# Layers multiplied in couples of 64 rows, one per half of the tokens, with each unit's second turn behind the next unit's first

## The chip, the cores and the metric

The kernel runs on one core of one Trainium2 chip. The metric is the device time of one execution in microseconds (us). The median of 3 runs of the kernel before is 607.14 us (607.09 to 607.23).

Engines are named as in the profile: PE is TensorE's matrix multiplier and PEld its loading of weights, DVE is VectorE, ACT is ScalarE, POOL is GpSimd, and SP is the engine whose queue issues the DMAs here.

## The reference

A causal attention is followed by two layers with gates and squares. In short, with batch 2, 12 heads, 448 positions, head size 64, so 896 tokens of 768 channels:

```
scores = q @ k.T / sqrt(64), masked above the diagonal
attn   = exp(scores - max) / (sum + 1e-9)
x      = attn @ v, as 896 x 768
g      = x @ w_gate                      # 768 x 1536
y      = (g * sigmoid(g) * (x @ w_val)) @ w_out      # 1536 x 768
h      = y @ w_in                        # 768 x 2048
out    = (max(h, 0) ** 2) @ w_out2       # 2048 x 768
```

q, k and v are float32; the weights are float64 and are read from memory as pairs of 32-bit words.

## The kernel before

The attention comes first (lines 655 to 662). Its order on all engines is written by a planner (`attention_plan`), and two of its parts matter here. Lines 496 to 498 multiply the scores of two heads as a couple: one head's data lies in rows 0 to 63 of the tiles and the other's in rows 64 to 127, and each goes to a bank of its own. And the planner also splits the first weights and multiplies the first half of the tokens of units 0 and 1 early (tiles `early`, line 635).

The layers work in *units*, the list `units` of lines 287 to 297. A unit is a set of 128 x 768 weights: `g` and `v` are the gate and value weights for 128 of 1536 channels (24 units, in turns g, v, g, v), `o` is half of the contraction for 128 channels of y (12 units, two per m), `h` is 128 channels of the second hidden layer (16 units), `f` is a stretch of the last product (16 units).

For each unit, SP loads 768 KB of raw weights (`load_w`, line 319). Then `split_w` makes two float32r tiles of them, `whi` (the high part) and `wlo` (what is left of it), in nine steps: ACT takes the absolute value (L337) and copies the high part (L352), and DVE does L340, L345, L349, L355, L359, L362 and L365; the last of these writes `wlo`. L359 is the last to read the raw tile, and so frees it for another load. `split_to` interleaves the steps of one unit with the first steps of the next, and puts *follow-ups* between them: work on earlier results that waits in the list `later` (sigmoid, products, copies out of PSUM).

A product of float32 precision is three matmuls of float32r: high weights by high part of the activations, high by low, low by high (`mm3`, lines 590 to 598). Each is done for both halves of the tokens (448 each), which have a PSUM bank each. A unit of g, v, o or h is six blocks of 128 rows, so 6 x 3 x 2 = 36 matmuls of 128 rows and 448 columns. Each of them loads its weights itself. The last layer (line 766) uses the activations as weights and 384 columns, and stays as it is.

What sets the order in the layers is the order in which the code is written: on each engine instructions run as they were issued. `unit` (line 406) splits up to the next unit's weights, issues loads, and returns this unit's weights; then come its matmuls; its follow-ups are put into `later` and are issued between the steps of the next split. There are 8 PSUM banks; a bank is taken again after eight others.

Of the kernel before, what the change touches and what calls it, by code (L numbers as in the profile page):

```python
# [16 lines left out]
ALU = mybir.AluOpType  # L17
PSUM = bass.MemoryType.PSUM

# [219 lines left out]
def tile_attention_moe_moe(ctx, tc, q, k, v, w_gate, w_val, w_out, w_in2, w_out2, out):  # L239
# [17 lines left out]
    wsp_p = ctx.enter_context(tc.tile_pool(name="wsp", bufs=3))  # L257
# [32 lines left out]
    for m in range(KD):  # L290
        units += [("o", m, 0), ("o", m, 1)]
# [127 lines left out]
    def halves(b):  # L419
        return slice(b * S, (b + 1) * S)  # L420
# [178 lines left out]

    def gate_or_val(kind, m, bs):  # L600
        hi, lo = unit(kind, m, 0)
        pss = {b: bank(kind) for b in bs}
        for kk in range(KD):
            c = slice(kk * 128, (kk + 1) * 128)
            mm3(pss, hi[:, c], lo[:, c], x_hi[kk], x_lo[kk], kk == 0, kk == KD - 1)
        return pss
# [42 lines left out]
    with tc.manual_schedule():  # L649
# [43 lines left out]
        for m in range(KF1):  # L693
            for kind in "gv":
                ps = gate_or_val(kind, m, [1] if n < NEARLY else [0, 1])
                if n < NEARLY:
                    ps[0] = early[n]
                n += 1
                if kind == "g":
                    later += [partial(sigmoids, ps), *(partial(times, sg, ps[z], z) for z in range(B))]  # L700
                else:
                    later.append(lambda: None)
                    for z in range(B):
                        later += [partial(times, up, ps[z], z), partial(gated, m, z)]
# [4 lines left out]
        for m in range(KD):  # L709
            pss = {b: bank("y") for b in range(B)}  # L710
            for j in range(2):
                hi, lo = unit("o", m, j)
                n = KF1 // 2
                for kk in range(n):
                    c = slice(kk * 128, (kk + 1) * 128)
                    f = j * n + kk
                    mm3(pss, hi[:, c], lo[:, c], g_hi[f], g_lo[f], f == 0, f == KF1 - 1)

            def first_part(m, pss):
                for b in range(B):  # L720
                    nc.scalar.activation(out=y_hi[m][:, halves(b)], in_=pss[b][:, :S], func=AF.Copy)

            def rest(m, pss, b):
                hs = halves(b)
                nc.vector.tensor_tensor(
                    out=y_lo[m][:, hs], in0=pss[b][:, :S], in1=y_hi[m][:, hs].bitcast(F32),
                    op=ALU.subtract)

            later += [partial(first_part, m, pss), partial(rest, m, pss, 0), partial(rest, m, pss, 1)]
# [4 lines left out]
        for m in range(KF2):  # L734
            hi, lo = unit("h", m, 0)
            pss = {b: bank("h") for b in range(B)}
            for kk in range(KD):
                c = slice(kk * 128, (kk + 1) * 128)
                mm3(pss, hi[:, c], lo[:, c], y_hi[kk], y_lo[kk], kk == 0, kk == KD - 1)
            u = {}  # L740
# [14 lines left out]
            later += [partial(squares, m, pss, u), partial(rest, m, u, 0), partial(rest, m, u, 1)]  # L755
# [4 lines left out]
        for half in range(2):  # L760
# [17 lines left out]
            for t in range(NTK):  # L778
                o = tmp_p.tile([128, N], F32, tag="osb", name="osb", bufs=6)
                if t % 2:  # L780
                    nc.vector.tensor_copy(out=o, in_=pss[t][:, :N])
                else:
                    nc.scalar.activation(out=o, in_=pss[t][:, :N], func=AF.Copy)
                nc.sync.dma_start(
                    out=out[t * 128:(t + 1) * 128, half * N:(half + 1) * N], in_=o)
# [30 lines left out]
```

## Time and profile before

| what | value |
|---|---|
| median of 3 runs | 607.14 us |
| the profiled execution's own time | 606.39 us |
| its span, first to last instruction | 604.6 us |
| granted TensorE clock | 1.00 |
| PE busy | 598.3 us, 99% |
| DVE busy | 479.2 us, 79% |
| ACT busy | 280.0 us, 46% |
| POOL busy | 91.9 us, 15% |

The profile is of one execution. A busy PE isn't PE at its peak: matmuls are pipelined and their ends are modelled, so the time that one takes in a stream is read from the starts of two, not from its length. In the timeline a row gives start and length in us, engine, line, operation, output and inputs by the program's names, shapes and the count of equal instructions merged into the row; brackets hold the engine's idle time ahead of it and what ended this. Names of tiles are shared by several uses: `b` in a row of o or h is an activation tile, `y` is the bank that o writes.

### The profile page before, as it was taken

How to read it: one execution, taken by the hardware profiler on the slowest of the kernel's cores; microseconds unless marked ns; L12 is line 12 of the kernel's file. 1: busy time of each engine (PE TensorE's matmuls, PEld its weight loads, DVE VectorE, ACT ScalarE, POOL GpSimd, SP SyncE). 2: the span in 40 equal slices, each digit the busy share in tenths (PEclk: the TensorE clock that was granted, in tenths of full speed). 3: DMA queues.
4: the chain of work that ended last, by engine and by line, in shares of the span. 5: the costliest groups of instructions: out<-in, count | busy, mean ns of one | idle time of the engine just before them, and what ended most of it. 6: DMA issues, size and time to landing. Idle time of an engine off the chain costs nothing.

```text
span 604.6 us, 8813 instructions
## 1 busy us (share of the span) xinstructions
PE 598.3 (99%) x3257; PEld 531.7 (88%) x3258; DVE 479.2 (79%) x843; ACT 280.0 (46%) x544; POOL 91.9 (15%) x161
## 2 busy tenths in 40 slices
PE   8999999999999999999999999999999999999997
PEld 5667667999999999999999999999999999999997
DVE  4779994888999999999977776888888888649741
ACT  5889883433333333333422224666666642222201
POOL 6556573111111111111000000000000000000000
PEclk9999999999999999999999999999999999999999
DMA  7776210333333333333433333333333335345202
GB/s 162 163 195 159 84 53 2 106 104 105 104 105 105 105 105 104 105 105 107 155 105 105 104 105 105 106 105 105 105 104 106 104 106 157 104 134 139 82 1 91
DMA packets 80778, 65.05 MB, mean 108 GB/s; under 512 B 34912, under 2 KB 76640, under 8 KB 80736
## 3 DMA queue, kind: packets, MB, share of 16 engines
q1 hardware_dynamic: 80736, 64.50, 36.2%
q8 instruction: 25, 0.41, 0.3%
q14 instruction: 17, 0.14, 0.1%
HBM read 61.73 MB, written 2.75 MB: 107 GB/s over the span
## 4 chain that ended last, share of the span: by engine, by line
PE 97%; POOL 1%; DMA 0%; SPq 0%; issue 0%; DVE 0%; ACT 0%; ACTq 0%; POOLq 0%
PE o L766 19%; PE h L598 7%; PE h L596 7%; PE h L594 7%; PE y L596 5%; PE y L594 5%; PE y L598 5%; PE v L594 5%; PE g L594 5%; PE g L596 5%; PE v L596 5%; PE v L598 5%; PE g L598 5%; PE s L498 4%; PE x L573 3%; PE pt L544 3%
## 5 line engine op out<-in xcount | busy, mean ns | idle before, releaser
L352 ACT ACTIVATE whi<-wa 128x768 fp32r<-128x768 f32 x68 | 57.6, 847 | 177.6 <-DVE wa L349 135.1
L766 PE MATMUL o<-whi,b 128*128 128x384 f32 x336 | 85.6, 334 | 0.0
L340 DVE TENSOR_SCALAR wa<-wa 128x768 f32<-128x768 f32 x68 | 41.4, 608 | 45.9 <-ACT wa L337 45.9
L349 DVE SCALAR_TENSOR_TENSOR wa<-wraw,wa 128x768 uint32<-128x768 uint32 x68 | 75.6, 1112 | 0.1
L337 ACT ACTIVATE wa<-wraw 128x768 f32<-128x768 f32 x68 | 61.7, 907 | 17.8 <-DVE wlo L365 17.8
L365 DVE TENSOR_TENSOR wlo<-wa,wr 128x768 fp32r<-128x768 f32 x68 | 65.6, 965 | 0.1
L362 DVE TENSOR_TENSOR wa<-wa,whi 128x768 f32<-128x768 f32 x68 | 64.6, 950 | 0.4 <-ACT whi L352 0.4
L359 DVE SCALAR_TENSOR_TENSOR wr<-wraw,wr 128x768 f32<-128x768 uint32 x68 | 64.6, 950 | 0.0
L766 PEld LDWEIGHTS o<-whi,b 128*128 128x128 f32 x336 | 60.7, 188 | 0.0
L766 PE MATMUL o<-wlo,b 128*128 128x384 f32 x168 | 56.2, 334 | 0.0
L598 PE MATMUL h<-b,wlo 128*128 128x448 f32 x192 | 55.2, 368 | 0.0
L594 PE MATMUL h<-b,whi 128*128 128x448 f32 x192 | 55.2, 368 | 0.0
L689 POOL TENSOR_TENSOR b<-u,b 128x448 fp32r<-128x448 f32 x24 | 29.0, 1207 | 159.2 <-ACT b L688 159.2
L534 POOL TENSOR_SCALAR P<-P,st 128x448 f32<-128x448 f32 (+1 forms) x96 | 50.5, 545 | 12.2 <-DVE st L526 9.2
L516 ACT ACTIVATE P<-P,st 128x192 f32<-128x192 f32 (+3 forms) x96 | 47.6, 498 | 7.4 <-DVE st L510 4.8
L596 PE MATMUL y<-b,whi 128*128 128x448 f32 x144 | 41.4, 368 | 0.0
L598 PE MATMUL y<-b,wlo 128*128 128x448 f32 x144 | 41.4, 368 | 0.0
L594 PE MATMUL y<-b,whi 128*128 128x448 f32 x144 | 41.4, 368 | 0.0
L596 PE MATMUL g<-alo,whi 128*128 128x448 f32 x138 | 40.2, 368 | 0.0
L596 PE MATMUL v<-alo,whi 128*128 128x448 f32 x138 | 40.2, 368 | 0.0
L594 PE MATMUL v<-ahi,whi 128*128 128x448 f32 x138 | 40.2, 368 | 0.0
L594 PE MATMUL g<-ahi,whi 128*128 128x448 f32 x138 | 40.2, 368 | 0.0
(97 smaller groups left out, 1152.7 us busy)
## 6 DMA issues: line engine op xcount, KB each, us to landing
wraw<-in_moe_w_out_dram SPq DMA_DIRECT2D x28, 768.0 KB, 4.4
wraw<-in_moe_w_in_dram SPq DMA_DIRECT2D x16, 768.0 KB, 4.6
wraw<-in_moe_w_gate_dram SPq DMA_DIRECT2D x12, 768.0 KB, 4.3
wraw<-in_moe_w_val_dram SPq DMA_DIRECT2D x12, 768.0 KB, 4.4
raw<-in_q_dram SPq DMA_DIRECT2D x24, 112.0 KB, 2.7
raw<-in_k_dram SPq DMA_DIRECT2D x24, 112.0 KB, 2.9
out_dram<-osb SPq DMA_DIRECT2D x14, 192.0 KB, 1.9
v<-in_v_dram SPq DMA_DIRECT2D x24, 96.0 KB, 2.7
```

The lines of the kernel that those rows point to most:

```text
L337: nc.scalar.activation(out=af, in_=high.bitcast(F32), func=AF.Abs)
L349: nc.vector.scalar_tensor_tensor(out=a, in0=high, scalar=0xC0000000, in1=a, op0=ALU.bitwise_and, op1=ALU.bitwise_or)
L352: nc.scalar.activation(out=split_t[n][0], in_=af, func=AF.Copy)
L359: nc.vector.scalar_tensor_tensor(out=rf, in0=low, scalar=2.0 ** -52, in1=rf, op0=ALU.mult, op1=ALU.mult)
L362: nc.vector.tensor_tensor(out=af, in0=af, in1=split_t[n][0].bitcast(F32), op=ALU.subtract)
L365: nc.vector.tensor_tensor(out=split_t[n][1], in0=af, in1=r[0].bitcast(F32), op=ALU.add)
L516: nc.scalar.activation(out=a, in_=a, func=AF.Exp, scale=-1.0, bias=st(0), accum_out=st(1))
L534: nc.gpsimd.tensor_scalar(out=o, in0=a, scalar1=st(2), scalar2=1.0, op0=ALU.mult, op1=ALU.mult)
L594: nc.tensor.matmul(out=pss[b][:, :S], lhsT=hi, rhs=mhi[:, halves(b)], start=first, stop=False)
L596: nc.tensor.matmul(out=pss[b][:, :S], lhsT=hi, rhs=mlo[:, halves(b)], start=False, stop=False)
L598: nc.tensor.matmul(out=pss[b][:, :S], lhsT=lo, rhs=mhi[:, halves(b)], start=False, stop=last)
L766: nc.tensor.matmul(out=pss[t][:, :N], lhsT=a[f][:, tk], rhs=w[:, c], start=f + n == 0, stop=f == KF2 - 1 and n == 2)
```

## The change

A product of g, v, o and h is now made in two *turns*. In each turn every block of 128 rows is multiplied as couples: a matmul with rows 0 to 63 for one half of the tokens, and one with rows 64 to 127 for the other half. In turn 0 rows 0 to 63 go to the first half's bank, in turn 1 they go to the second half's. So a unit has 2 x 18 couples, 72 matmuls instead of 36, each with a load of its own. In a turn a bank is written by one half of the rows alone.

A bank changes from one half of the rows to the other between the two turns. `product` issues a unit's first turn, then a no-op on SP that waits for the turn's last two matmuls, and then the *second turn of the unit before*. The first two matmuls of a second turn wait for the no-op of their own unit. The second turn of a stage's last unit is issued at the stage's end (`second_turn()` calls).

Units 0 and 1 of g and v stay as they were. In o the units come in another order: for two m at a time, first the two units with j = 0, then the two with j = 1, and for j = 1 the first turn has the rows of j = 0's second one. There are now four buffers for split weights instead of three, and four for output tiles instead of six.

```diff
@@ -16,6 +16,7 @@
 AF = mybir.ActivationFunctionType
 ALU = mybir.AluOpType
 PSUM = bass.MemoryType.PSUM
+AFTER = mybir.DependencyInfo(mybir.DependencyClass.Sync, mybir.DependencyReason.DATA)
 
 
 W_TINY = 2.0 ** (896 // 8 - 127)
@@ -254,7 +255,7 @@
     const = ctx.enter_context(tc.tile_pool(name="const", bufs=1))
     wraw_p = ctx.enter_context(tc.tile_pool(name="wraw", bufs=3))
     dec_p = ctx.enter_context(tc.tile_pool(name="wdec", bufs=1))
-    wsp_p = ctx.enter_context(tc.tile_pool(name="wsp", bufs=3))
+    wsp_p = ctx.enter_context(tc.tile_pool(name="wsp", bufs=4))
     ax_p = ctx.enter_context(tc.tile_pool(name="ax", bufs=1))
     early_p = ctx.enter_context(tc.tile_pool(name="early", bufs=1))
     ps_p = ctx.enter_context(tc.tile_pool(name="ps", bufs=8, space=PSUM))
@@ -287,8 +288,8 @@
     units = []
     for m in range(KF1):
         units += [("g", m, 0), ("v", m, 0)]
-    for m in range(KD):
-        units += [("o", m, 0), ("o", m, 1)]
+    for m in range(0, KD, 2):
+        units += [("o", m + z, j) for j in range(2) for z in range(2)]
     for m in range(KF2):
         units.append(("h", m, 0))
     FU = KF2 // 2
@@ -597,6 +598,47 @@
         for b in bs:
             nc.tensor.matmul(out=pss[b][:, :S], lhsT=lo, rhs=mhi[:, halves(b)], start=False, stop=last)
 
+    open_turns = []
+
+    def turn(t, ws, pss, xs, first, last, ready=None):
+
+        mms = []
+        for kk, (mhi, mlo) in enumerate(xs):
+            c = slice(kk * 128, (kk + 1) * 128)
+            for z, (w, a) in enumerate(((0, mhi), (0, mlo), (1, mhi))):
+                for r in range(2):
+                    b, rows = r ^ t, slice(64 * r, 64 * r + 64)
+                    mms.append(nc.tensor.matmul(
+                        out=pss[b][:, :S], lhsT=ws[w][rows, c], rhs=a[rows, halves(b)],
+                        start=first and kk == z == 0, stop=last and kk == len(xs) - 1 and z == 2))
+        if ready:
+            for mm in mms[:2]:
+                tc.add_manual_dep(mm.ins, ready.ins.name, AFTER, reason="banks change rows")
+        return mms[-2:]
+
+    def second_turn():
+        for args, done in open_turns:
+            turn(*args)
+            later.extend(done)
+        open_turns.clear()
+
+    def product(key, pss, xs, first=True, last=True, done=()):
+
+        t, n = int(not first), units.index(key)
+        split_to(n + 2)
+        ws = split_t[n]
+        mms = turn(t, ws, pss, xs, first, False)
+        ready = nc.sync.nop()
+        for mm in mms:
+            tc.add_manual_dep(ready.ins, mm.ins.name, AFTER, reason="banks change rows")
+        load_w(n + 5)
+        second_turn()
+        open_turns.append(((1 - t, ws, pss, xs, False, last, ready), done))
+
     def gate_or_val(kind, m, bs):
         hi, lo = unit(kind, m, 0)
         pss = {b: bank(kind) for b in bs}
@@ -692,52 +734,53 @@
         n = 0
         for m in range(KF1):
             for kind in "gv":
-                ps = gate_or_val(kind, m, [1] if n < NEARLY else [0, 1])
                 if n < NEARLY:
+                    ps = gate_or_val(kind, m, [1])
                     ps[0] = early[n]
+                else:
+                    ps = {b: bank(kind) for b in range(B)}
+                if kind == "g":
+                    done = [partial(sigmoids, ps), *(partial(times, sg, ps[z], z) for z in range(B))]
+                else:
+                    done = [lambda: None]
+                    for z in range(B):
+                        done += [partial(times, up, ps[z], z), partial(gated, m, z)]
+                if n < NEARLY:
+                    later += done
+                else:
+                    product((kind, m, 0), ps, list(zip(x_hi, x_lo)), done=done)
                 n += 1
-                if kind == "g":
-                    later += [partial(sigmoids, ps), *(partial(times, sg, ps[z], z) for z in range(B))]
-                else:
-                    later.append(lambda: None)
-                    for z in range(B):
-                        later += [partial(times, up, ps[z], z), partial(gated, m, z)]
+        second_turn()
 
 
 ...
+        half = KF1 // 2
+        for m in range(0, KD, 2):
+            both = [{b: bank("y") for b in range(B)} for z in range(2)]
             for j in range(2):
-                hi, lo = unit("o", m, j)
-                n = KF1 // 2
-                for kk in range(n):
-                    c = slice(kk * 128, (kk + 1) * 128)
-                    f = j * n + kk
-                    mm3(pss, hi[:, c], lo[:, c], g_hi[f], g_lo[f], f == 0, f == KF1 - 1)
-
-            def first_part(m, pss):
-                for b in range(B):
-                    nc.scalar.activation(out=y_hi[m][:, halves(b)], in_=pss[b][:, :S], func=AF.Copy)
-
-            def rest(m, pss, b):
-                hs = halves(b)
-                nc.vector.tensor_tensor(
-                    out=y_lo[m][:, hs], in0=pss[b][:, :S], in1=y_hi[m][:, hs].bitcast(F32),
-                    op=ALU.subtract)
-
-            later += [partial(first_part, m, pss), partial(rest, m, pss, 0), partial(rest, m, pss, 1)]
+                for z, pss in enumerate(both):
+                    product(
+                        ("o", m + z, j), pss, list(zip(g_hi, g_lo))[j * half:(j + 1) * half], j == 0, j == 1,
+                        [partial(first_part, m + z, pss), *(partial(rest, m + z, pss, b) for b in range(B))]
+                        if j else [])
+        second_turn()
 
 
         free = x_hi[4:] + x_lo + extra[:24]
         r_hi, r_lo = free[0:32:2], free[1:32:2]
         for m in range(KF2):
-            hi, lo = unit("h", m, 0)
-            pss = {b: bank("h") for b in range(B)}
-            for kk in range(KD):
-                c = slice(kk * 128, (kk + 1) * 128)
-                mm3(pss, hi[:, c], lo[:, c], y_hi[kk], y_lo[kk], kk == 0, kk == KD - 1)
-            u = {}
+            pss, u = {b: bank("h") for b in range(B)}, {}
 
             def squares(m, pss, u):
                 for b in range(B):
@@ -752,7 +795,9 @@
                 nc.vector.tensor_tensor(
                     out=r_lo[m][:, hs], in0=u[b], in1=r_hi[m][:, hs].bitcast(F32), op=ALU.subtract)
 
-            later += [partial(squares, m, pss, u), partial(rest, m, u, 0), partial(rest, m, u, 1)]
+            product(("h", m, 0), pss, list(zip(y_hi, y_lo)), done=[
+                partial(squares, m, pss, u), *(partial(rest, m, u, b) for b in range(B))])
+        second_turn()
 
 
         N = DM // 2
@@ -776,7 +821,7 @@
                 for z, t in order:
                     add_up(hi, lo, u, z, t)
             for t in range(NTK):
-                o = tmp_p.tile([128, N], F32, tag="osb", name="osb", bufs=6)
+                o = tmp_p.tile([128, N], F32, tag="osb", name="osb", bufs=4)
                 if t % 2:
                     nc.vector.tensor_copy(out=o, in_=pss[t][:, :N])
                 else:

```

The functions `first_part` and `rest` of o stand ahead of its loop now, unchanged.

In the rows that follow, lines are those of the kernel they come from: after the change `turn` multiplies in L615, and the lines of the split and the follow-ups are one or some more (L366 for L365, L726 for L684).

On PE, at a border in g and v. Before: the end of a v unit (banks v_1692 and v_1693, weights whi_1588 and wlo_1589) and the start of the next g unit.

```order
L596 MATMUL v_1692<-alo5_88,whi_1588 128x448
L596 MATMUL v_1693<-alo5_88,whi_1588 128x448
L598 MATMUL v_1692<-ahi5_82,wlo_1589 128x448
L598 MATMUL v_1693<-ahi5_82,wlo_1589 128x448
L594 MATMUL g_1753<-ahi0_77,whi_1626 128x448 [waits Activation_49]
L594 MATMUL g_1754<-ahi0_77,whi_1626 128x448
L596 MATMUL g_1753<-alo0_83,whi_1626 128x448
L596 MATMUL g_1754<-alo0_83,whi_1626 128x448
L598 MATMUL g_1753<-ahi0_77,wlo_1627 128x448 [waits DVE_49]
L598 MATMUL g_1754<-ahi0_77,wlo_1627 128x448
```

After, for the border of a later pair: the end of a g unit's first turn (banks g_1956 and g_1957), the start of the second turn of the v unit before it, and its continuation.

```order
L615 MATMUL g_1956<-alo5_88,whi_1782 128x448
L615 MATMUL g_1957<-alo5_88,whi_1782 128x448
L615 MATMUL g_1956<-ahi5_82,wlo_1783 128x448
L615 MATMUL g_1957<-ahi5_82,wlo_1783 128x448
L615 MATMUL v_1859<-ahi0_77,whi_1686 128x448 [waits SP_sequencer_49]
L615 MATMUL v_1858<-ahi0_77,whi_1686 128x448
L615 MATMUL v_1859<-alo0_83,whi_1686 128x448
L615 MATMUL v_1858<-alo0_83,whi_1686 128x448
L615 MATMUL v_1859<-ahi0_77,wlo_1687 128x448
L615 MATMUL v_1858<-ahi0_77,wlo_1687 128x448
```

Where the next unit's matmuls followed, the second turn of the unit before now follows; its couples take the banks in the other order (1859 first), and its first matmul waits for SP.

On DVE, while the weights of unit 4 are split (`wlo_1627` before, `wlo_1629` after), with unit 2's follow-ups before (`sg` is made of the bank g_1633 and g_1634):

```order
L355 TENSOR_SCALAR wr_1679<-wa_1612 128x768
L340 TENSOR_SCALAR wa_1673<-wa_1673 128x768
L359 SCALAR_TENSOR_TENSOR wr_1679<-wraw_1546,wr_1679 128x768
L345 TENSOR_SCALAR wa_1673<-wa_1673 128x768
L684 TENSOR_TENSOR sg_1675<-g_1633,sg_1675 128x448
L362 TENSOR_TENSOR wa_1612<-wa_1612,whi_1626 128x768
L349 SCALAR_TENSOR_TENSOR wa_1673<-wraw_1570,wa_1673 128x768
L684 TENSOR_TENSOR sg_1677<-g_1634,sg_1677 128x448
L365 TENSOR_TENSOR wlo_1627<-wa_1612,wr_1679 128x768
```

and after, up to the follow-ups of the same unit 2 (banks g_1610 and g_1611), which now stand with unit 5's split (`wlo_1687`):

```order
L363 TENSOR_TENSOR wa_1614<-wa_1614,whi_1628 128x768
L350 SCALAR_TENSOR_TENSOR wa_1676<-wraw_1570,wa_1676 128x768
L366 TENSOR_TENSOR wlo_1629<-wa_1614,wr_1678 128x768
L356 TENSOR_SCALAR wr_1772<-wa_1676 128x768
L341 TENSOR_SCALAR wa_1766<-wa_1766 128x768
L360 SCALAR_TENSOR_TENSOR wr_1772<-wraw_1570,wr_1772 128x768
L346 TENSOR_SCALAR wa_1766<-wa_1766 128x768
L726 TENSOR_TENSOR sg_1768<-g_1610,sg_1768 128x448
L363 TENSOR_TENSOR wa_1676<-wa_1676,whi_1686 128x768
L350 SCALAR_TENSOR_TENSOR wa_1766<-wraw_1612,wa_1766 128x768
L726 TENSOR_TENSOR sg_1770<-g_1611,sg_1770 128x448
L366 TENSOR_TENSOR wlo_1687<-wa_1676,wr_1772 128x768
```

The two products of `sg` moved from ahead of unit 4's low part to ahead of unit 5's; the same holds for all later follow-ups of g and v.

## Rows read from the trace of the kernel before

**Rows 1.** The page: busy time, share of the span and instructions of each engine.

```profile
PE 598.3 (99%) x3257; PEld 531.7 (88%) x3258; DVE 479.2 (79%) x843; ACT 280.0 (46%) x544; POOL 91.9 (15%) x161
```

**Rows 2.** By stretch: length, PE, PEld, DVE, ACT, POOL busy, clock, DMA.

```profile
112.20:275.90 163.70, 163.70 (x794) 148.74 (x793) 148.32 (x200) 60.30 (x89) 26.62 (x22) 1.00 0.33 106
...
365.20:484.20 119.00, 119.00 (x578) 108.12 (x577) 98.60 (x143) 78.55 (x125) 0.00 (x0) 1.00 0.35 104
```

**Rows 3.** Timeline of PE: starts of unit 2, o and h.

```profile
112.20 0.57 PE L594 MATMUL g<-ahi,whi 128*128 128x448 f32 x2
...
275.88 0.57 PE L594 MATMUL y<-b,whi 128*128 128x448 f32 x2
...
365.16 0.57 PE L594 MATMUL h<-b,whi 128*128 128x448 f32 x2
```

**Rows 4.** Timeline of PE: three bf16 matmuls in the attention.

```profile
10.00 0.82 PE L275 MATMUL qk<-warm 128*128 128x512 bf16 x3
```

**Rows 5.** Groups by line: the same matmuls, count, busy us and mean ns.

```profile
L275 PE MATMUL qk<-warm 128*128 128x512 bf16 x7 | 2.2, 382 | 0.0
```

**Rows 6.** Timeline of PE and PEld: transposes, then the scores' couples.

```profile
62.82 0.55 PE L474 MATMUL qk<-ident,raw 112*128 112x112 f32 x4
...
63.11 0.26 PE L474 MATMUL qk<-ident,raw 112*128 112x112 f32 x1
63.30 0.19 PEld L498 LDWEIGHTS s<-qk 64*128 64x128 f32 x2
...
63.40 0.19 PEld L498 LDWEIGHTS s<-qk 64*128 64x128 f32 x2
...
63.78 0.81 PE L498 MATMUL s<-qk 64*128 64x448 f32 x4
...
64.15 0.70 PE L498 MATMUL s<-qk 64*128 64x320 f32 x4
...
64.42 0.60 PE L498 MATMUL s<-qk 64*128 64x320 f32 x4
```

**Rows 7.** Timeline of DVE in g and v: L340, two units apart.

```profile
180.78 0.83 DVE L340 TENSOR_SCALAR wa<-wa 128x768 f32<-128x768 f32 x1 [0.97 <-ACT wa L337]
...
195.57 0.82 DVE L340 TENSOR_SCALAR wa<-wa 128x768 f32<-128x768 f32 x1 [0.98 <-ACT wa L337]
```

**Rows 8.** Timeline of DVE: low parts of units 3, 23, 25, 62, 63.

```profile
117.77 1.91 DVE L365 TENSOR_TENSOR wlo<-wa,wr 128x768 fp32r<-128x768 f32 x1
...
266.55 0.94 DVE L365 TENSOR_TENSOR wlo<-wa,wr 128x768 fp32r<-128x768 f32 x1
...
281.32 0.94 DVE L365 TENSOR_TENSOR wlo<-wa,wr 128x768 fp32r<-128x768 f32 x1
...
553.02 0.95 DVE L365 TENSOR_TENSOR wlo<-wa,wr 128x768 fp32r<-128x768 f32 x1
...
554.96 0.56 DVE L340 TENSOR_SCALAR wa<-wa 128x768 f32<-128x768 f32 x1 [0.38 <-ACT wa L337]
...
558.51 0.95 DVE L365 TENSOR_TENSOR wlo<-wa,wr 128x768 fp32r<-128x768 f32 x1
```

**Rows 9.** Timeline of ACT and DVE: last y tile, o to h.

```profile
365.15 0.98 ACT L721 ACTIVATE b<-y 128x448 fp32r<-128x448 f32 x2 [4.09 <-PE y L598]
...
368.00 0.62 DVE L725 TENSOR_TENSOR ahi<-y,b 128x448 fp32r<-128x448 f32 x1
```

**Rows 10.** DMA issues: queue, count, KB each, median us from issue to landing.

```profile
wraw<-in_moe_w_gate_dram SPq DMA_DIRECT2D x12, 768.0 KB, 4.3
...
out_dram<-osb SPq DMA_DIRECT2D x14, 192.0 KB, 1.9
```

**Rows 11.** The chain that ended last, in order of time: the f stage.

```profile
484.36 116.50 PE o L766 x672
```

**Rows 12.** Timeline of PE: second and ninth of unit 0's early matmuls.

```profile
90.49 0.37 PE L596 MATMUL early<-alo,whi 128*128 128x448 f32 x1
...
91.90 0.37 PE L598 MATMUL early<-ahi,wlo 128*128 128x448 f32 x1
```

More of the change, by code (lines that the diff above doesn't have):

```diff
@@ L707, in tile_attention_moe_moe, with first_part @@
+        second_turn()
         y_hi = extra[24:30]
         y_lo = extra[30:32] + x_hi[:4]
-        for m in range(KD):
-            pss = {b: bank("y") for b in range(B)}
-            for j in range(2):
-                hi, lo = unit("o", m, j)
-                n = KF1 // 2
-                for kk in range(n):
-                    c = slice(kk * 128, (kk + 1) * 128)
-                    f = j * n + kk
-                    mm3(pss, hi[:, c], lo[:, c], g_hi[f], g_lo[f], f == 0, f == KF1 - 1)
-            def first_part(m, pss):
-                for b in range(B):
-                    nc.scalar.activation(out=y_hi[m][:, halves(b)], in_=pss[b][:, :S], func=AF.Copy)
-            def rest(m, pss, b):
-                hs = halves(b)
-                nc.vector.tensor_tensor(
-                    out=y_lo[m][:, hs], in0=pss[b][:, :S], in1=y_hi[m][:, hs].bitcast(F32),
-                    op=ALU.subtract)
-            later += [partial(first_part, m, pss), partial(rest, m, pss, 0), partial(rest, m, pss, 1)]
+        def first_part(m, pss):
+            for b in range(B):
+                nc.scalar.activation(out=y_hi[m][:, halves(b)], in_=pss[b][:, :S], func=AF.Copy)
@@ new lines, in rest @@
+        def rest(m, pss, b):
+            hs = halves(b)
+            nc.vector.tensor_tensor(
+                out=y_lo[m][:, hs], in0=pss[b][:, :S], in1=y_hi[m][:, hs].bitcast(F32),
+                op=ALU.subtract)
+        half = KF1 // 2
+        for m in range(0, KD, 2):
+            both = [{b: bank("y") for b in range(B)} for z in range(2)]
+            for j in range(2):
+                for z, pss in enumerate(both):
[3 more added lines that the diff above has]
+                        if j else [])
```

## The prediction

> **What bounds the kernel now.** I read the shares of the span first, then the busy time by stage, then where each stage starts, then what VectorE waits for. TensorE is busy 99% of the span [rows 1]. After the attention there are four stages without a hole: g and v to 275.9, o to 365.2, h to 484.2, f to the end. In a stage TensorE's busy time is the whole window, at a granted clock of 1.00, the 2.4 GHz level [rows 2]. So a stage lasts as long as its matmuls: o takes 365.16 - 275.88 = 89.28 us for 432 matmuls of 448 columns, 0.2067 each; g and v from 112.20 take 163.68 for 792, again 0.2067 [rows 3]. A unit is 36 of them, 7.44 us; h, 16 units, ends at 365.16 + 119.04 = 484.20.
>
> Two other kinds of matmul run at a better pace. Three bf16 matmuls of 512 columns take 0.82 [rows 4], of which the last one's own length is 0.38 [rows 5]: they start (0.82 - 0.38)/2 = 0.22 apart; scaled to 448 columns that is 0.19. And the attention's scores already run as couples of 64 rows: the second couple of 448 columns stands from 63.78 to 64.15, 0.37, the first of 320 columns from there to 64.42, 0.27 [rows 6]. These fp32 products take two passes, each at half the rate, so a full-rate pass would take half of 0.37: 0.187. Each such couple is two matmuls with two loads, and the row of one window holds both couples, four matmuls: a couple's two run at once. So 0.0167 us of 0.2067, 8%, is what couples might give back in g, v, o and h. In f nothing is coupled.
>
> VectorE is the second thing to see. From 112.2 to 275.9 it is busy 148.3 of 163.7 us [rows 2]. The same instruction of its chain, L340, behind the same wait for ACT, stands at 180.78 and at 195.57: 14.79 for two units, against 14.88 on TensorE [rows 7]. It isn't TensorE that holds it: both times it had waited for ACT's Abs, 0.97 and 0.98. Without follow-ups its chain takes 558.51 - 553.02 = 5.49 per unit [rows 8]; so the follow-ups of one g and one v cost 14.79 - 10.98 = 3.81.
>
> **The change part by part.**
> *Couples.* 22 units of g and v, 12 of o and 16 of h, 36 matmuls each, become 36 couples each: 72 matmuls and 72 loads. No row has fp32r couples of 64 rows. From below: 0.187, half of the score couple. From above: 0.21, if a couple's two loads follow one another; loads on one half of the rows are 0.10 apart (63.30, 63.40) [rows 6]. Between them lies 0.2067, if what costs the 0.02 is not the change of weights. I take 0.190, nearest to the couples of rows 6. A turn is 18 couples, 3.42 us, a unit 6.84.
>
> *Order of turns.* A unit's first turn waits for its split weights; its second comes after the next unit's first turn, and so after the next unit's weights. Follow-ups reach VectorE one unit later: ahead of a given low part stand the follow-ups of one unit fewer, some 1.9 us (half of 3.81).
>
> *g and v.* Here VectorE sets the pace, 7.39 a unit, whatever a couple takes. In the trace the low part of the last unit (number 23) ends at 266.55 + 0.94 = 267.49 [rows 8]. Less 1.9, and less 0.38 since the turn's third couple is the first to need it, the turn starts at 265.2. Three turns follow (first of 23, second of 22, second of 23), 10.26, so the stage ends at 275.5 instead of 275.88. Gain 0.4.
>
> *o.* Unit 25 again waits for its low part. Before, this ended at 281.32 + 0.94 = 282.26 [rows 8]; less 1.9, plus some 0.4 because the last two units' follow-ups come together: 280.8, turn at 280.4. One more wait of 0.7 (estimated) at unit 26, then VectorE has few follow-ups and TensorE sets the pace: unit 35 starts at 280.4 + 0.7 + 10 x 6.84 = 349.5, and three turns later o ends at 359.8, against 365.16. Gain 5.4.
>
> *h.* VectorE's work is 98.6 us over 16 units, 6.2 each [rows 2], with 0.38 of waiting for ACT [rows 8]: 6.5, under 6.84, so TensorE sets the pace with little to spare. The first unit needs the last y tile after 15 of 18 couples, 2.85 us, where it had 6.2. From the start of ACT's copy to the end of the second half of y's low part took 368.00 + 0.62 - 365.15 = 3.5 [rows 9], with split work between that will now have been done; I put 0.3 for it. 359.8 + 0.3 + 16 x 6.84 = 469.5, against 484.2. Gain 14.7 in all.
>
> *Bank order by SP.* The no-op waits for a first turn. Ahead of it on SP stands a load that waits for L359 of the next unit, which the next unit's first turn needs anyway, and the second turn comes only after that one. Cost nothing; the cover is one turn, 3.4 us. Queued behind it are only loads; one lands in 4.3 us [rows 10] and is wanted units later. If the cover failed, each second turn would wait for as much as it failed by.
>
> *Buffers.* A fourth pair of split weights holds the open turn. Four output buffers instead of six: a group of the last f unit is 6 matmuls of 0.173, 1.04 us, so the fifth output is wanted 4.2 us after the first, and one lands in 1.9 [rows 10]. Cost nothing. f keeps its 116.5 us [rows 11].
>
> Sum on the profiled execution: span 604.6 - 14.7 = 589.9. That execution took 606.39, the median of the runs is 607.14; the same gain taken from the median gives 592.4. With 0.187 a couple the same steps give -17.4, 589.7; with 0.200, -5.5, 601.6; nothing is gained at about 0.204.
>
> **Rivals.**
> 1. *A couple takes as long as a full-row matmul: slower.* The 0.02 may belong to streaming fp32r at full rate. For it: f, with 384 columns, runs at 116.50/672 = 0.1734 [rows 11], which is 0.013 above 384/448 of 0.187, so the excess shrinks with the columns and is no fixed price per load; and the early matmuls, same shape and loads, ran seven steps in 91.90 - 90.49, 0.201 each [rows 12]. Against: nothing in [rows 4, 6] shows such an excess. Then the new order costs: TensorE has only unit 2's first turn (112.2 to 115.9) and stands still until the low part of unit 3, 117.77 + 1.91 = 119.7 [rows 8], so unit 3 starts at 119.3. From there 20 units of 7.44 and three turns of 3.72 end g and v at 279.3, 3.4 late, and nothing returns it: +3.7 with the 0.3 before h, 610.8. It decides from 0.204 a couple upward.
> 2. *Loads in series.* A couple takes 0.214 if its two loads don't overlap. For it: twice as many loads. Against: [rows 6] have two loads at 63.30 and two at 63.40. With units of 7.70 g and v end at 119.3 + 154.1 + 11.6 = 284.9, o at 377.4, h at 501.0: +16.8, 623.9.
> By the Trainium skill, page "TensorE: Matmul & The Clock Gate", section "LDWEIGHTS (loading the stationary operand)", a load's time goes by its columns and not by its rows, so a load of 64 rows is no shorter than one of 128: the page speaks against the change, which doubles the loads. The 0.10 between loads of 64 rows agrees; with both halves' loads in series the sum is rival 2's 623.9, with the halves side by side, as rows 6 have them, the forecast's 592.4.
> 3. *A hole at each change of turn.* At the change from transposes to couples the last transpose starts at 63.11 and the first couple at 63.30, 0.19, where transposes are (0.55 - 0.26)/3 = 0.10 apart [rows 6]. A hole of 0.09 at both turns of 28 units costs 5.0: 597.4. Against: each turn here has the same form as the last.
>
> **How the numbers follow.** Forecast, 0.187 to 0.197 a couple: 0.48; rival 3 or a couple near 0.200: 0.11; rival 1 and its neighbours: 0.27; rival 2 and worse: 0.14. No change within 0.2% (1.2 us, about what a measurement of this kernel can tell) needs a couple of 0.203 to 0.205: 0.06, out of rival 1's edge. So faster 0.59, same 0.06, slower 0.35. The likeliest case's own range is 588 to 600; with both signs in it the range is 587 to 614.
>
> **What would show it.** Couple pace: in h equal couples start 0.19 apart and h takes 110 us; 119 means rival 1, 123 rival 2. VectorE's pace: in g and v TensorE now waits once a unit for the low part (L365's), some 0.5 each, and the stage still ends near 275; if it ends much earlier, my reading of VectorE's chain is wrong. Bank order: TensorE never waits for SP. What would overturn the forecast is the couple: all its gain lies in o and h.

## The result and the profile after

The change makes the kernel slower by 0.7%: 611.53 us in the median (610.97 to 612.36) against 607.18 (607.09 to 607.23) beside it, a ratio of 1.0073 with a 95% interval of 1.0055 to 1.009. The forecast was 592.4, so the direction is wrong. The time lies in the range (587 to 614) only because that range held a gain and a loss alike. What came is rival 1, whose sum was 610.8. Where runs are compared, the medians are of fast executions; two slow ones of e_buffers, at 833 and 1499 us, are left out.

The profiled execution of after took 610.97 us, its span is 609.2 at a granted clock of 1.00. Its page, in the columns of [rows 1], then a group of its costliest ones (columns: busy us, mean ns of one, idle time before them and what ended it):

```profile
PE 599.7 (98%) x5057; PEld 531.2 (87%) x5058; DVE 478.8 (79%) x843; ACT 281.1 (46%) x544; POOL 91.9 (15%) x161
...
L615 PE MATMUL v<-ahi,wlo 64*128 64x448 f32 x264 | 48.7, 366 | 3.0 <-DVE wlo L366 3.0
```

PE's busy time is not smaller, as a gain would need, but 1.4 us larger, and there is now an idle place of 3.0 us that before had none. Where it is, the timeline of PE shows (start and length in us; x2 is a couple, x4 two of them):

```profile
112.65 0.48 PE L615 MATMUL g<-ahi,whi 64*128 64x448 f32 x2
...
116.68 0.38 PE L615 MATMUL v<-alo,whi 64*128 64x448 f32 x2
120.10 0.47 PE L615 MATMUL v<-ahi,wlo 64*128 64x448 f32 x2 [3.04 <-DVE wlo L366]
...
121.02 0.37 PE L615 MATMUL v<-ahi,whi 64*128 64x448 f32 x2
...
123.50 0.37 PE L615 MATMUL g<-ahi,whi 64*128 64x448 f32 x2
...
279.74 0.57 PE L615 MATMUL y<-b,whi 64*128 64x448 f32 x4
...
369.02 0.57 PE L615 MATMUL h<-b,whi 64*128 64x448 f32 x4
```

Two things are to be seen. After unit 2's first turn (from 112.65) TensorE starts on unit 3 and stands still until its low part is there. And behind it couples start 0.2067 apart: 12 from 121.02 to 123.50 in 2.48 us. The stages' starts stand against [rows 3]: unit 2 0.45 late, o 3.86 late, h 3.86 late. So 3.41 us are lost in g and v, and nothing comes back. The 0.45 ahead of unit 2 is no more than two executions of one kernel differ by: the two traces of e_first, below, start unit 2 at 112.19 and at 112.80. The chain of waits, in order of time (start, us, engine, tile, count), says the same by lengths:

```profile
131.10 7.44 PE v L615 x72
...
279.90 89.28 PE y L615 x864
369.18 119.04 PE h L615 x1152
488.22 116.72 PE o L811 x672
```

A unit of g and v is 7.44, as before. o is 89.28 us, which is 365.16 - 275.88 of [rows 3] to the hundredth, with 864 matmuls in place of 432. h is the 119.04 that the prediction worked out for before. f has 0.22 more than in [rows 11]. PE's timeline shows 0.2 of it where couples give way to full rows: f's first matmul starts 0.30 behind the last couple and the next 0.28 behind it, where 0.21 and 0.17 are usual. f now ends at 604.94, before at 600.86, 4.1 late. The last 0.5 of the span's 4.6 lies behind the last matmul. Here is the last copy out, in ACT's timeline of after:

```profile
605.01 0.49 ACT L828 ACTIVATE osb<-o 128x384 f32<-128x384 f32 x1 [1.59 <-PE o L811]
```

It waited for PE, not for an output buffer, and the span ends 3.7 us after it. Why this end is longer stays open: from the last matmul to the end of the span it is 3.9 to 4.3 us in the five traces of the change's kernels, and 3.4 to 3.8 in before, e_bump, e_512, e_384, e_once, e_short and e_four.

### The profile page after: what moved, and what is told of

Read it like the earlier page. It is cut to its first block, busy times and chain, and to the rows that moved or that the text cites. A ratio compares the mean times of both kernels' runs of the same rounds, so it can differ in the third digit from the quotient of the medians.

```text
span 609.2 us, 12455 instructions
## 1 busy us (share of the span) xinstructions
PE 599.7 (98%) x5057; PEld 531.2 (87%) x5058; DVE 478.8 (79%) x843; ACT 281.1 (46%) x544; POOL 91.9 (15%) x161
## 4 chain that ended last, share of the span: by engine, by line
PE 96%; DVE 2%; POOL 1%; ACT 1%; issue 0%; ACTq 0%; POOLq 0%
PE h L615 20%; PE o L811 19%; PE y L615 15%; PE v L615 13%; PE g L615 13%; PE s L499 4%; PE x L574 3%; PE pt L545 3%; PE qk L475 2%; PE pt L550 1%; POOL P L535 1%; PE idle L276 1%; DVE wlo L366 0%; PE pt L555 0%; PE early L595 0%
## 5 line engine op out<-in xcount | busy, mean ns | idle before, releaser
L615 PE MATMUL h<-b,whi 64*128 64x448 f32 x512 | 84.0, 365 | 0.0
L615 PE MATMUL y<-b,whi 64*128 64x448 f32 x576 | 82.8, 365 | 0.0
L615 PE MATMUL h<-b,wlo 64*128 64x448 f32 x384 | 70.7, 365 | 0.0
L366 DVE TENSOR_TENSOR wlo<-wa,wr 128x768 fp32r<-128x768 f32 x68 | 65.7, 967 | 0.1
L615 PEld LDWEIGHTS y<-b,whi 64*128 64x128 f32 x576 | 54.0, 184 | 5.5
L615 PE MATMUL y<-b,wlo 64*128 64x448 f32 x288 | 53.0, 365 | 0.0
L615 PEld LDWEIGHTS h<-b,whi 64*128 64x128 f32 x512 | 47.9, 184 | 4.9
L615 PE MATMUL v<-ahi,wlo 64*128 64x448 f32 x264 | 48.7, 366 | 3.0 <-DVE wlo L366 3.0
L615 PE MATMUL g<-alo,whi 64*128 64x448 f32 x264 | 48.7, 365 | 0.0
L615 PE MATMUL g<-ahi,whi 64*128 64x448 f32 x264 | 48.7, 366 | 0.0
```

The source lines that it names most:

```text
L366: nc.vector.tensor_tensor(out=split_t[n][1], in0=af, in1=r[0].bitcast(F32), op=ALU.add)
L615: mms.append(nc.tensor.matmul(out=pss[b][:, :S], lhsT=ws[w][rows, c], rhs=a[rows, halves(b)], start=first and kk == z == 0, stop=last and ...
```

## The experiments

The theory after the result: 0.020 of the 0.2067 belongs to float32r streaming, whatever its loads and rows, so the split into rows can't give it back, and the new order costs its stand-still. Rivals: it belongs to the loads (which the change doubled, so that a gain and a loss might cancel), or to the data or the banks; or the loss is spread over the turns.

**p1_widths: which widths pay the 0.02?** The loop of each unit of h was replaced by

```diff
+            W = WIDTHS[m]
+            n = max(36, 2 * int(3900 / max(W / 2.4, 107)))
+            for z in range(n):
+                kk, b = z // 2 % KD, z % 2
+                w = max(S, W) if z < 2 else W
+                o = b * (NT - w)
+                nc.tensor.matmul(
+                    out=pss[b][:, :w], lhsT=hi[:, kk * 128:(kk + 1) * 128], rhs=y_hi[kk][:, o:o + w],
+                    start=z < 2, stop=z >= n - 2)
```

> The kernel before, with each of the 16 units of h replaced by a stream of 36 or more full-row float32r matmuls of one width, which changes from unit to unit (448, 384, 512, 256, 416, 320, 480, 288, 224, 352, 192, 304, 400, 128, 272, 448 columns); so h is not the reference's and its time means nothing. Read: the distance between starts in each unit. Theory A, the 0.02 us beyond columns / 2.4 GHz is a fixed price for each matmul or load: 256 columns take 0.127, 320 take 0.153, 512 take 0.233. Theory B, the price grows with the streamed columns, as the two widths known so far suggest (448: 0.2067, 384: 0.1734, 0.52 ns a column): 256 take 0.107, 320 take 0.140, 512 take 0.240. In A narrower matmuls lose, in B three of 299 columns in place of two of 448 win 6%.

Below are timeline rows of PE, each cut out of one unit's stream, and the groups by shape with the mean ns of one matmul, its own length. The *pace* is the distance between two starts: (length of the row - own length) / (count - 1).

```profile
365.81 7.39 PE L744 MATMUL h<-b,whi 128*128 128x448 f32 x35
374.74 6.57 PE L744 MATMUL h<-b,whi 128*128 128x384 f32 x37
383.70 6.51 PE L744 MATMUL h<-b,whi 128*128 128x512 f32 x28
391.77 5.44 PE L744 MATMUL h<-b,whi 128*128 128x256 f32 x44
475.73 5.52 PE L744 MATMUL h<-b,whi 128*128 128x128 f32 x48
492.31 7.05 PE L744 MATMUL h<-b,whi 128*128 128x448 f32 x34
```

```profile
L744 PE MATMUL h<-b,whi 128*128 128x448 f32 x99 | 22.4, 367 | 0.0
L744 PE MATMUL h<-b,whi 128*128 128x256 f32 x70 | 8.6, 283 | 0.0
...
L744 PE MATMUL h<-b,whi 128*128 128x512 f32 x36 | 8.4, 390 | 0.0
...
L744 PE MATMUL h<-b,whi 128*128 128x384 f32 x46 | 8.1, 334 | 0.0
...
L744 PE MATMUL h<-b,whi 128*128 128x128 f32 x70 | 7.9, 274 | 0.0
```

So (7.39 - 0.367)/34 = 0.2066 at 448 columns, 0.1732 at 384, 0.2267 at 512, 0.1199 at 256, and 0.1116 at 128, where something else than the columns decides. Over columns / 2.4 GHz that is 0.0132 at 256 and 384 and 0.0134 at 512. The price doesn't grow with the columns, so theory B (0.107 at 256) falls; it is near to fixed, as in theory A, but at some 0.0133 and not 0.020. The other widths from 256 to 512 lie around it: 272 columns, the least, pay 0.012, and 480, the most, 0.017. Only 448 is out of line with 0.020, and in the last row, the same kind of matmul at the end of the sweep, it runs at (7.05 - 0.367)/33 = 0.2025, 0.016 over: 448 columns have two paces.

**p2_kinds: what does the price hang on?** As p1, at 448 columns, with one kind for each unit (other weights, data, rows or columns in the same loop).

> The kernel before, with each unit of h replaced by 40 matmuls of one kind at 448 columns: plain full rows; weights of zeros; data of zeros; one PSUM bank for all instead of two in turn; bf16; one matmul of 64 rows alone; couples of 64 rows; couples of 384 columns; loads of 32 and of 64 columns. h is not the reference's. Theory S (the 0.02 us belongs to streaming float32r at full rate, whatever the load): 64 rows alone, couples and loads of 32 or 64 columns all take 0.207, bf16 0.19. Theory L (it belongs to the load of 128 columns that stands between two matmuls): loads of 32 columns take 0.19, and bf16 takes 0.207 as well. Theory D (it depends on what is multiplied): zeros take 0.19. Theory P (on changing the bank): one bank takes another time than two. Couples: 0.2067 in S and L; 384-column couples 0.173.

Timeline of PE and the group of bf16, as above (float32r's mean is 0.363 to 0.369); the rows are zero weights, plain, bf16, plain behind bf16, 64 rows alone, couples, loads of 32 columns:

```profile
374.66 7.60 PE L772 MATMUL h<-b,b 128*128 128x448 f32 x36
...
415.78 7.39 PE L772 MATMUL h<-b,whi 128*128 128x448 f32 x35
424.84 6.41 PE L772 MATMUL h<-hb 128*128 128x448 bf16 x33
...
439.71 7.46 PE L772 MATMUL h<-b,whi 128*128 128x448 f32 x36
448.22 7.05 PE L772 MATMUL h<-b,whi 64*128 64x448 f32 x34
464.77 6.51 PE L772 MATMUL h<-b,whi 64*128 64x448 f32 x62
...
480.76 6.43 PE L772 MATMUL h<-b,whi 128*32 128x448 f32 x31
```

```profile
L772 PE MATMUL h<-hb 128*128 128x448 bf16 x72 | 14.0, 353 | 0.0
```

Weights of zeros take (7.60 - 0.37)/35 = 0.2066 like the plain unit behind them (data of zeros and one bank did too): D and P fall. bf16 takes (6.41 - 0.353)/32 = 0.1893. Everything after the bf16 stream is at the lower pace: plain (7.46 - 0.367)/35 = 0.2027, 64 rows alone (7.05 - 0.363)/33 = 0.2026, loads of 32 columns 0.2022; 31 couples have 61 gaps in 6.15 us, 0.1008 each, 0.202 a couple. A load with a quarter of the columns and half the rows in use change nothing, so theory L, a load of 128 columns, falls, and S stands: the price goes with streaming float32r. Each matmul here has a load of its own, so a price of any load in float32r, whatever its size, is not excluded. What I had not expected is that the pace changed, to the end of h, after something else than a 448-column float32r matmul had stood between.

**e_first and e_direct: what does the order cost, what does it save?**

```diff
 # e_first, behind unit 2's product(...)
+                    if n == NEARLY:
+                        second_turn()
 # e_direct, at the end of product
+        second_turn()
```

> The kernel after, but unit 2's second turn follows its own first at once, so TensorE has 3.7 us more to do before unit 3's low part. If the loss is the stand-still at unit 3 (my rival 1's mechanism), it shrinks from 3.0 to under 0.3, a hole of some 0.3 to 0.5 at the change of rows comes in, and the time is 608.4 to 609.0. If the loss is spread over the turns (waits on SP, loads, the mode), it stays at 611.5.

Timeline of PE in e_first, and a window behind the wait (columns as in [rows 2]):

```profile
124.03 0.37 PE L615 MATMUL g<-alo,whi 64*128 64x448 f32 x2
127.46 0.69 PE L615 MATMUL g<-ahi,wlo 64*128 64x448 f32 x2 [3.07 <-DVE wlo L366]
127.95 0.58 PE L615 MATMUL g<-ahi,whi 64*128 64x448 f32 x2
...
131.16 0.36 PE L615 MATMUL g<-ahi,whi 64*128 64x448 f32 x2
...
141.49 0.57 PE L615 MATMUL g<-ahi,whi 64*128 64x448 f32 x2
```

```profile
127.50:131.00 3.50, 3.50 (x20) 3.15 (x22) 3.09 (x5) 0.87 (x1) 0.00 (x0) 0.51 0.01 2
```

My expectation failed: the wait didn't shrink, it moved to unit 4 (3.07). One turn of lead is what the order takes, wherever it is taken: the next first turn asks for the next low part a turn earlier. In this trace too the loss is one stand-still, not spread. The two matmuls of a couple needn't keep one pace: from 131.16 to 141.49, 51 couples, the row of a couple grows from 0.36 to 0.57. So one matmul of each couple went at 0.2026 and the other 0.0041 slower, at 0.2067. The 12 times fell into two groups, four of 605.3 to 606.3 and eight of 612.2 to 613.4 (median 612.53, ratio 1.0058, 1.0025 to 1.0091). A second trace was taken for that:

> The kernel after with unit 2's second turn behind its own first, again, for a second trace: its times fell into two groups, 605.3 to 606.3 and 612.2 to 613.4. If the groups are the two paces, a trace near 606 has couples 0.2026 apart in all stages (1800 x 0.0041 = 7.4 us), and one near 613 has them 0.2067 apart from some unit on.

It came out at 613.0, with a wait of 3.21 at unit 4 and its couples 0.2067 apart from 133 us on. The faster group was not caught in a trace.

> The kernel after, but every unit's second turn follows its own first at once: no unit is open while another begins. Theory T (the order by SP is free only because a turn of 3.7 us lies between): each of the 50 units pays a hole, the drain of the last couple and two semaphores by way of SP, some 0.3 to 0.5 each, so 608 + 15 to 25 = 623 to 633, and the wait for unit 3's low part is gone. Rival: the change of rows costs nothing even at once; then it is 607.5 to 608.5, and the order of turns was the only thing that the change lost by.

621.23 us, ratio 1.0239 (1.0226 to 1.0252): T's mechanism, 1.8 us under its range, and the wait for unit 3's low part is gone. The timeline of PE at a change of rows within one unit of o:

```profile
300.86 0.37 PE L615 MATMUL y<-b,wlo 64*128 64x448 f32 x2
301.33 0.68 PE L615 MATMUL y<-b,whi 64*128 64x448 f32 x4
301.84 0.36 PE L615 MATMUL y<-b,wlo 64*128 64x448 f32 x2
...
304.27 0.37 PE L615 MATMUL y<-b,wlo 64*128 64x448 f32 x2
```

The last couple and the first of the second turn stand 0.47 apart instead of 0.20, and the next two take 0.51 instead of 0.41: a hole of 0.37. Behind it 12 couples take 2.43, 0.2025 each. By the starts in the trace the lower pace follows 41 of the 50 holes, and 0.2067 the other nine. Where the lower pace comes, it returns 36 x 0.0041 = 0.15 of the price and leaves 0.22. In all that is 50 x 0.37 - 41 x 0.15 = 12.4 us; the medians (621.23 and 606.99) differ by 14.2. With a turn of another unit between, no such hole shows in after, where o and h are a count of couples times 0.2067: that part of the change does what it says.

**e_384: does VectorE pace g and v?**

```diff
 # the second of mm3's three; the third likewise, the first (W3) but for a bank's first matmul
-            nc.tensor.matmul(out=pss[b][:, :S], lhsT=hi, rhs=mlo[:, halves(b)], start=False, stop=False)
+            nc.tensor.matmul(out=pss[b][:, :384], lhsT=hi, rhs=mlo[:, b * S:b * S + 384], start=False, stop=False)
```

> The kernel before, with only the first 384 columns of each half in all matmuls of g, v, o and h but the first of a bank; so the results of the other 64 tokens of each half are wrong. A unit costs TensorE 6.3 us instead of 7.44, as if couples had been 15% faster. If VectorE paces g and v at 7.39 a unit (the prediction), that stage still ends at 275 or later; if it doesn't, it ends near 251. o and h: 12 and 16 units of 6.25 if TensorE sets the pace (75 and 100 us); if VectorE does in h, 6.5 a unit, 104.

576.52 us. What PE waited for in g and v (us in total, times, longest), the starts of unit 2 and o in PE's timeline, and in DVE's the same step of two units of h that follow one another:

```profile
PE g L601 <- DVE wlo L365: 12.9, 11, 1.2
PE v L601 <- DVE wlo L365: 4.3, 11, 0.4
```

```profile
110.18 0.57 PE L597 MATMUL g<-ahi,whi 128*128 128x448 f32 x2
...
272.32 0.57 PE L597 MATMUL y<-b,whi 128*128 128x448 f32 x2
```

```profile
402.85 0.56 DVE L340 TENSOR_SCALAR wa<-wa 128x768 f32<-128x768 f32 x1 [0.39 <-ACT wa L337]
...
409.40 0.56 DVE L340 TENSOR_SCALAR wa<-wa 128x768 f32<-128x768 f32 x1 [0.39 <-ACT wa L337]
```

22 units take 162.1 us, 7.37 each, with a wait in each, though TensorE needs only 6.3: the prediction's 7.39 holds. The stage ends at 272.3, not at 275 or later, since it began 2.0 earlier and is 1.5 shorter than in [rows 3]. With matmuls 15% faster those 1.5 us are what g and v had to give. In h VectorE's step comes every 6.55 us and sets the pace of the later units, 6.5 to 6.6 each; h takes 102.9 us, from 350.58 to 453.48.

**e_buffers** has `bufs=4` for `wsp` and for `osb`, in before.

> The kernel before with four buffers of split weights instead of three and four output tiles instead of six, and nothing else of the change. Prediction's step: cost nothing, 607.0 within 0.3. If buffers made part of the loss, 608 or more.

606.96 against 606.60, ratio 1.0004 (0.9995 to 1.0014): no cost that can be told from none.

**e_bump, e_512: can the stream be put into its lower pace, or cut into better widths?** A *bump* is one bf16 matmul of zeros, put between float32r matmuls only to disturb their stream.

```diff
 # e_bump: in o for each m, in h for each unit
+            nc.tensor.matmul(out=pss[0][:, :S], lhsT=bump[:, :128], rhs=bump, start=True, stop=True)
 # e_512: banks of 512 and 384 columns in o and h
+CUT = 512
...
+        return slice(0, CUT) if b == 0 else slice(CUT, NT)
```

> The kernel before, with one bf16 matmul of 448 columns (zeros, into the bank that the unit's own first matmul then starts afresh) ahead of each m of o and each unit of h. Theory M: a stream of 448-column float32r matmuls has two paces, 0.2067 and 0.2026 a matmul, and keeps the one it is in until something else stands between; in the probe of kinds the full-row stream behind a bf16 stream ran at 0.2026. Then the 28 units of o and h go to 0.2026 at least in part: 1008 x 0.0041 = 4.1 us gained, 22 bumps of some 0.2 lost, up to 607.0 + 4.4 - 4.1, so about 607, but with starts 0.2026 apart in the trace of o and h. If the pace belongs to the kind alone (0.2026 in the probe came from elsewhere), starts stay 0.2067 apart and the time is 611.4.

606.62 against 606.60, ratio 1.0001 (0.9992 to 1.0009): theory M, with starts 0.2026 apart in o and h, and gain and price in balance.

> The kernel before, with the 896 tokens cut at 512 instead of 448 in o and h (one bank takes 512 columns, the other 384); full rows. Theory M: 448 columns pay 0.020 over columns / 2.4 GHz where other widths pay about 0.0135 (384 0.0133, 512 0.0142 in the sweep of widths), so a pair takes 0.2275 + 0.1733 = 0.4008 instead of 0.4133: 28 units x 18 pairs x 0.0125 = 6.3 us, 600.7. Rival: alternating widths don't keep the paces of their own streams (each change disturbs), and a pair takes 0.405 to 0.413: 603 to 607.

606.90, ratio 1.0007 (0.9998 to 1.0016): the rival. In its chain o and h last exactly as long as with equal halves:

```profile
276.07 89.28 PE y L600 x432
365.35 119.04 PE h L600 x576
```

89.28/216 = 0.4133 for a pair, not the 0.4008 of the expectation, or the 0.1732 + 0.2267 = 0.400 that the rows of p1_widths add up to. So the higher pace isn't the width's alone; a sweep of equal widths doesn't tell what a mixture does.

**e_once, e_short, e_four: one bump a stage?** Before's kernel with `bump(pss[0])` (a bf16 matmul of zeros, started and stopped) ahead of a few units:

```diff
+        if m == 1 and kind == "g": bump(pss[0])      # e_once; o and h: if m == 0
+        if 0 in bs: bump(pss[0])                     # e_short, 64 columns; o and h: every m
+        if m % 2 == 1 and kind == "g": bump(pss[0])  # e_four; o and h: if m == 0
```

> The kernel before, with three bf16 matmuls of 448 columns in all: ahead of unit 2 (g), of the first unit of o and of the first unit of h. Theory M (two paces, and the stream keeps its pace until disturbed): o and h run at 0.2026 a matmul throughout, 1008 x 0.0041 = 4.1 us less; g and v go down to VectorE's pace, 7.31 a unit by the run with 384 columns, 22 x 0.13 = 2.9 us at most, 1.1 with the 7.39 of the trace before; three bumps cost 0.6. So 600 to 602. If the lower pace lasts only a unit or two and each bump only buys 72 matmuls, as the run with a bump for each unit leaves open, the gain is some 0.3 a stage less the bumps: 606 to 607.

602.7 us, ratio 0.9923 (0.9909 to 0.9936), 0.7 above the range of theory M. The bumps of o and h in its PE timeline, and windows of g and v behind the bump and later:

```profile
276.08 0.36 PE L274 MATMUL y<-bf 128*128 128x448 bf16 x1
...
363.84 0.36 PE L274 MATMUL h<-bf 128*128 128x448 bf16 x1
...
480.78 0.34 PE L776 MATMUL o<-whi,ahi 128*128 128x384 f32 x1
```

```profile
112.80:137.50 24.70, 24.70 (x124) 22.90 (x124) 21.95 (x30) 9.65 (x15) 5.50 (x4) 1.00 0.31 97
145.00:276.00 131.00, 131.00 (x636) 118.86 (x634) 118.85 (x161) 48.10 (x72) 21.10 (x18) 1.00 0.34 109
```

o takes 363.84 - 276.08 = 87.76 us with its bump, h 116.94: 0.2026 x 432 and x 576 and 0.24 for a bump each, against 89.28 and 119.04. One bump holds for a whole stage of 576 matmuls. In g and v it held for some 28 us (24.7 for the 122 whole ones of 124 in the first window, 0.2025); from 145 on it is 131.0/634 = 0.2066 again, which is what the forecast missed. The granted clock is 1.00 at both paces, so this isn't the clock.

> The kernel before, with a bf16 matmul of 64 columns ahead of each unit of g and v from unit 2 on, of each m of o and of each unit of h: 44 bumps. If a short bump moves the stream to the lower pace as the one of 448 columns did (which cost 0.21 each), and costs some 0.1: 36 x 50 x 0.0041 = 7.4 less 4.4, with VectorE's floor in g and v 602 to 604. If a bump has to be of the full width, starts stay 0.2067 apart and it is 611.

603.96, ratio 0.9955 (0.9943 to 0.9968): a bump of 64 columns works as well (by the starts in the trace the lower pace follows each of the 44), but 44 of them cost more than they add.

> The kernel before with a bf16 matmul of 448 columns ahead of every fourth unit of g and v (from unit 2 on), and of the first units of o and h. In the run with one ahead of unit 2, g and v kept 0.2027 for some 26 us (3.5 units) and then went back to 0.2067. Four units now take 4 x 7.30 + 0.2 = 29.4 instead of 29.76, less where VectorE's 7.31 to 7.39 a unit decides: 1.1 to 2 us under the run with three bumps (602.7), 600.7 to 601.6. If VectorE's waits throw the stream back each time, 602.5 to 603.5.

601.06 us, ratio 0.991 (0.9894 to 0.9925): as worked out, the fastest version here, 0.9% under before with full rows and the old order.

**after_bump: have couples a better pace of their own?** The change's kernel with a 64-column bump ahead of unit 2's, o's and h's first turns.

> The kernel after, with a bf16 matmul of 64 columns ahead of the first turn of unit 2, of o's first unit and of h's first unit. Theory S+M (the price beyond columns / 2.4 GHz belongs to float32r streaming and has two sizes, for couples as for full rows): couples in o and h go to 0.2026, 1008 x 0.0041 = 4.1 us less, three bumps 0.4; in g and v the wait for unit 3's low part comes between and puts them back to 0.2067, so the 3.9 lost at the start stay: 607.8. If couples in the lower pace are faster than full rows in it (0.19 to 0.20), below 605. If two matmuls side by side can't be moved to the lower pace, 611.9.

607.64 (ten times of 606.67 to 612.00), ratio to before 1.0029 (1.0009 to 1.0049). The chain of the traced one (607.01), in order of time:

```profile
263.39 7.30 PE v L620 x72
...
278.11 89.47 PE y L620 x864
367.71 116.94 PE h L620 x1152
```

The time is as expected, but by luck, since other stages make it: behind the wait g and v are at 7.30 a unit, 36 x 0.2026, though they were expected at 0.2067; h is at 0.2026 as expected (116.94 = 1152/2 x 0.2026 + 0.24); and o, expected at 0.2026, stayed at 0.2067 in spite of its bump. Couples have the same two paces as full rows, and h is as long as in e_once. So the row split is worth nothing at either pace. The spread of the ten times may be stages that went to one pace or the other; no second trace shows it.

## Why the prediction was wrong

**The step that failed** is the pace of a couple: "Between them lies 0.2067, if what costs the 0.02 is not the change of weights. I take 0.190, nearest to the couples of rows 6." It measured 0.2067, so the gain of 14.7 us that was worked out with it came to nothing. The 0.187 came from halving the attention's fp32 couple, which has two passes of its own kind, and the bf16 row was scaled and taken for a full-rate stream in general. bf16 does run at 0.189 there. Over columns / 2.4 GHz float32r pays 0.012 to 0.017 at the other widths from 256 to 512 columns and 0.020 or 0.016 at 448, with 64 rows as with 128. The nearest row in kind was not the couple in [rows 6] but f's float32r in [rows 11], 0.0133 over its 0.160, and it stood in the prediction only as an argument for rival 1.

**Rival 1** was right in mechanism and size: TensorE stands still for unit 3's low part (3.04; forecast 3.4 between 115.9 and 119.3), g and v lose 3.41 (forecast 3.4), and h has the same length. That its sum of 610.8 is 0.7 from 611.53 is partly luck: its 0.3 ahead of h didn't come (h starts as late as o), while unit 2's 0.45, and 0.7 in f and at the end, were in no sum; 0.5 of this, behind the last copy, is not explained. Two of its arguments were half right. The excess doesn't shrink with the columns: 256, 384 and 512 pay the same. And [rows 12]'s 0.201 is near the lower pace, 0.2026, which the same shape and loads can have as well as 0.2067.

**g and v at VectorE's pace**: right, 7.37 in e_384 against 7.39. But it didn't come to bear, since couples were no faster: TensorE waited once and not once a unit.

**o and h**: nothing gained, since both are a count of matmuls times the pace. VectorE's estimate in h, 6.5 a unit, is 6.55 in e_384. The other two sums, -17.4 at 0.187 and -5.5 at 0.200, don't follow from the steps shown: 27.5 units of 36 couples, at 0.003 less or 0.010 more than 0.190, give -17.7 and -4.8 with all else as it stands.

**Bank order by SP**: cost nothing, as said, and e_direct shows its cover's worth: 0.37 a change without it. **Rivals 2 and 3** did not come: doubled loads are hidden (PEld 531.2 against 531.7 in [rows 1]), so they run side by side, and no hole shows at changes of turn, only the 0.2 where f follows couples.

By the Trainium skill, page "TensorE: Matmul & The Clock Gate", section "LDWEIGHTS (loading the stationary operand)", a load goes by its columns, not by its rows. The trace of p2_kinds agrees: loads of 64 rows took 184 ns in the mean and of 128 rows 188, while loads of 64 columns took 134 and of 32 columns 108. For the pace the load decided nothing: with 32 and 128 columns it was 0.2022 and 0.2027.

**Buffers**: right, 1.0004. **f**: 116.72 against 116.50.

What stays open: why 448 columns of float32r have two paces, what sends the stream from 0.2026 back to 0.2067 in g and v, why the bump ahead of o did nothing in after_bump, and why 512 with 384 also settles at 0.4133 a pair. That the faster group of e_first was all at the lower pace fits its distance (1800 couples x 0.0041 = 7.4) but no trace shows it.

## What to carry to other kernels

Price a new form of matmul from a row of the same data type and the same kind of stream; half of another type's pass is no evidence. Before a change doubles instructions to remove an excess, find out by a probe (widths, rows, load columns, type) which of them the excess hangs on. And an order that defers each second half by one unit pays its lead once, as a stand-still at the start, which only a later gain can pay back.

## What the runs showed of the hardware

A stream of 448-column float32r matmuls keeps one of two paces, 0.2067 or 0.2026 us, at the same granted clock of 1.00. In before's kernel the lower one followed each of the 77 bumps of e_bump, e_once, e_short and e_four (0.12 us for 64 columns, 0.2 for 448), and lasted up to 576 matmuls. Among couples it is less sure: it followed 41 of 50 holes of 0.37 in e_direct, and not the bump ahead of o in after_bump. Three bumps took before's kernel from 606.9 to 602.7, eight from 606.9 to 601.1.

Below 256 columns the pace of float32r stops falling: in p1_widths 224, 192 and 128 columns took 0.112 each, where columns / 2.4 GHz would be 0.093, 0.080 and 0.053.

After a stand-still of 3.07 us in e_first the granted clock was 0.51 over the next 3.5 us, the 1.2 GHz level, and couples stood 0.37 apart; after's 3.04 in the profiled execution left it at 1.00. So two nearly equal waits ended on either side. after's own four times may show the same: two of them, 611.96 and 612.36 us, have a mean granted clock of 0.996, and the other two, 610.97 and 611.10, of 1.00.
